# Dividing a seven-tap convolution between four engines in another way, in a fused convolution and gated-FFN kernel

**Chip, cores, metric.** One core of one Trainium2 chip. The metric is device time in microseconds (us) of one execution, first to last instruction of the core plus 1.7 to 1.9 us that the profile's span doesn't hold (785.21 us against a span of 783.3 in the kernel before). All runs quoted are fast (granted TensorE clock 0.98 or more, no outlier).

## The reference

```python
# x: (8, 4096, 192), weight: (8, 7), w_gate and w_val: (192, 1536), w_out: (1536, 192); all float32
w   = softmax(weight, axis=-1)                       # 8 heads x 7 taps
xc  = causal_conv_along_seq(x, w)                    # per head (24 channels), 6 zeros ahead of each batch row
xc  = xc.reshape(32768, 192)
g   = xc @ w_gate
out = (g * sigmoid(g) * (xc @ w_val)) @ w_out        # float32, (32768, 192)
```

## The kernel before

The 32768 tokens are 64 blocks of 512, four blocks to a unit, so 16 units (0 to 15). A block is 12 steps, j = 0 to 11; a step makes one gate and one val tile of 128x512 on TensorE, a SiLU of gate on ScalarE, h = SiLU x val on VectorE. At j = 1, 4, 7 and 10 TensorE also runs a phase of the down projection, which eats the h tiles of earlier steps.

The convolution of a unit is done ahead of its use, in one of two ways. Some units are convolved on TensorE, as matmuls with a banded matrix. The units in `POOLED` are convolved "channel-major": their input is cast to fp16 in DRAM (`xs`), loaded transposed (`x<-xs`, channels on partitions), and the seven taps become per-partition multiplies and adds, shared by VectorE, ScalarE and GpSimd. Each such unit has six jobs: four "block" jobs for channels 0 to 127 and two "pair" jobs for channels 128 to 191 of two blocks. Four placing copies for each block then put the result where TensorE reads it (`pxc`).

```python
POOLED = (3, 4, 5, 7, 8, 9, 11, 12, 13, 15)
...
    def turn_x(u, i, at):                       # a transposing load, on SyncE's queue
        rows = xs[u][TB * i : TB * i + TB + XP]
        ...
        t = cpool.tile([P, TB + XP], fp16, tag=tag, name=tag, bufs=6)     # rings of six: x0 and x64
        seq(nc.sync.dma_start_transpose(out=t, in_=rows[:, at : at + P]))
...
    SHARES = (                                  # taps on VectorE, ScalarE, GpSimd; jobs alternate
        ((0, 1), (2, 3, 4), (5, 6)),
        ((0, 1, 2), (3, 4), (5, 6)),
    )
...
            for k in pool_taps:                 # GpSimd: a multiply and an add for each of its taps
                part = cpool.tile([P, TB], fp32, tag="piece", name="piece", bufs=2)
                seq(nc.gpsimd.tensor_tensor(part, shifted(k),
                        job["tap"][:, k : k + 1].to_broadcast([P, TB]), op=ALU.mult))
                add(part, k)
...
    def place(u, i):                            # four copies on SyncE's queue
        t0, t1, t2 = xc[b]
        y = y2[u, i % 2][Q * (i // 2) : Q * (i // 2) + Q, :]
        for dst, src in (
            (t1[0:Q, 0:TB], t0[Q:P, 0:TB]), (t1[Q:P, 0:TB], y),
            (t2[0:Q, 0:TB], y), (t2[Q:P, 0:TB], t0[0:Q, 0:TB]),
        ):
            seq(nc.sync.dma_start(out=dst, in_=src))
...
    def pooled_work(n, room):                   # room: j in (1, 7, 10) and no TensorE convolution in this step
        if room:
            if on_dve: on_dve.pop(0)()          # one VectorE tap and one ScalarE tap of the oldest jobs
            if on_act: on_act.pop(0)()
        while placing: ...                      # place(u, i) once its jobs are 12 steps old
...
        silu[n] = seq(nc.scalar.activation(sg, g, AF.Silu)).ins           # in each step
        hj = hpool.tile([P, TB], fp16, tag="h", name="h", bufs=15)
        seq(nc.vector.tensor_tensor(hj, sg, v, op=ALU.mult))
...
            seq(nc.scalar.copy(o_sb[:, 0:2, :], acc[b][0]))               # at j = 4, then the store on SyncE
            seq(nc.vector.tensor_copy(o_sb[:, 2:4, :], acc[b][1]))
```

## Time and profile before

| | before |
|---|---|
| median (range) of the four runs beside the changed kernel | 787.86 us (784.68 to 788.2) |
| span of the profiled run, clock | 783.3 us, 1.00 |
| TensorE work of a block when nothing waits | 11.73 us |
| lost beyond that: blocks 0 to 5 / blocks 6 to 62 | 10.5 / 8.0 us |

The two last rows come from the start of the first gate matmul of each block. "Lost" is the distance between two such starts minus 11.73 us. The prediction shows the page's busy row, chain and main groups. Two more groups of that page matter for the move of the copies (columns: line, engine, operation, tiles, shapes, count | busy us, mean ns | idle before):

```profile
L778 DVE TENSOR_TENSOR h<-sig,val 128x512 f16<-128x512 f16 x768 | 498.7, 683 | 67.5 <-PE val L767 49.1
...
L852 DVE COPY o_sb<-acc 128x384 f32<-128x384 f32 x63 | 34.5, 548 | 0.0
L851 ACT COPY o_sb<-acc 128x384 f32<-128x384 f32 x63 | 30.2, 479 | 0.2
```

VectorE has h in every step, all its taps and one of two output copies, and is idle 67.5 us in 783 before h. TensorE's waits for other engines, the largest first (us in total, times, longest), are all short:

```profile
PE cv L462 <- DMA x<-x: 1.3, 1, 1.3
...
PE acc L793 <- DVE h L778: 0.7, 1, 0.7
```

### The profile page before, as it was taken

Reading aid. Unit: us, or ns where it says so; the run is one execution under the profiler, and the core shown is the slowest. Engines: PE = TensorE matmul, PEld = TensorE weight load, DVE = VectorE, ACT = ScalarE, POOL = GpSimd, SP = SyncE. Lnnn points to the kernel's source line nnn. Section 1 sums busy time; section 2 is a strip of 40 time slices with the busy share of each in tenths; the row PEclk is TensorE's granted clock in tenths of the full one; section 3 lists DMA queues with packets and bytes.
Section 4 is the critical chain, followed back from the end, with each engine's and each line's share of the span. In section 5 each row is a group of like instructions: output and inputs, shape, how many; then the busy total and the mean of one; then the engine's idle time right before and its main releaser. Section 6 shows DMA issues by size and latency. Waiting matters only on the chain.

```text
span 783.3 us, 28008 instructions
## 1 busy us (share of the span) xinstructions
PE 773.8 (99%) x11371; PEld 583.4 (74%) x11371; DVE 705.2 (90%) x1042; ACT 596.4 (76%) x1022; POOL 539.1 (69%) x459
## 2 busy tenths in 40 slices
PE   8999999999999999999999999999999999999998
PEld 5676667987888768888888866676787886666665
DVE  7676999999999989999999999999999988997775
ACT  6665877877877878778778778778787777786664
POOL 8200488988998769879899858788889965783000
PEclk9999999999999999999999999999999999999999
DMA  9996676652185465454156548555224753521211
GB/s 139 157 183 133 139 137 103 137 118 77 52 153 111 102 153 95 103 131 111 36 100 137 102 108 156 107 124 104 73 64 77 168 123 94 108 65 36 69 56 42
DMA packets 159803, 83.91 MB, mean 107 GB/s; under 512 B 102513, under 2 KB 159097, under 8 KB 159097
## 3 DMA queue, kind: packets, MB, share of 16 engines
q1 hardware_dynamic: 139144, 65.57, 36.5%
q0 software_dynamic: 20528, 16.55, 15.2%
q8 instruction: 89, 1.46, 0.8%
q14 instruction: 42, 0.34, 0.1%
HBM read 33.09 MB, written 38.60 MB: 92 GB/s over the span
## 4 chain that ended last, share of the span: by engine, by line
PE 93%; SPq 3%; DMA 2%; DVE 1%; issue 1%; POOL 1%; ACT 0%; DVEq 0%; POOLq 0%
PE gate L767 35%; PE acc L793 31%; PE val L767 26%; SPq L498 1%; SPq L520 1%; DMA x<-x 1%; DMA w<-in_moe_w_val_dram 1%; DVE h L778 1%; PE cv L462 1%; SPq L598 1%; POOL w L168 0%; PE acc L814 0%; POOL xe L98 0%; PE cv L373 0%; PE turn L431 0%
## 5 line engine op out<-in xcount | busy, mean ns | idle before, releaser
L776 ACT ACTIVATE sig<-gate 128x512 f16<-128x512 f32 x768 | 458.5, 597 | 168.0 <-PE val L767 76.7
L778 DVE TENSOR_TENSOR h<-sig,val 128x512 f16<-128x512 f16 x768 | 498.7, 683 | 67.5 <-PE val L767 49.1
L767 PEld LDWEIGHTS <-w 64*128 64x128 f16 x4608 | 317.4, 110 | 145.2 <-issue 3.1
L767 PE MATMUL gate<-pxc,w 64*128 64x512 f16 x1440 | 338.5, 376 | 0.0
L767 PE MATMUL val<-pxc,w 64*128 64x512 f16 x1440 | 337.0, 376 | 0.4
L793 PE MATMUL acc<-wo,h 64*128 64x192 f16 x6096 | 318.3, 243 | 0.7 <-DVE h L778 0.7
L793 PEld LDWEIGHTS <-h 64*128 64x128 f16 x6096 | 287.0, 94 | 39.5 <-issue 2.2
L634 POOL TENSOR_TENSOR total<-total,part 128x512 f32<-128x512 f32 x150 | 198.4, 1323 | 106.6 <-DVE total L668 69.8
L767 PE MATMUL gate<-xc,w 64*128 64x512 f16 x864 | 203.8, 376 | 0.5 <-ACT tap_c L567 0.5
L767 PE MATMUL val<-xc,w 64*128 64x512 f16 x864 | 203.5, 376 | 0.7 <-DMA w<-in_moe_w_val_dram 0.3
L649 POOL TENSOR_TENSOR piece<-x,tap_c 128x512 f32<-128x512 f16 x120 | 143.6, 1197 | 0.0
L681 ACT ACTIVATE part<-x,tap_c 128x512 f32<-128x512 f16 x150 | 107.1, 714 | 0.0
L668 DVE SCALAR_TENSOR_TENSOR total<-x,tap_c,total 128x512 f32<-128x512 f16 x90 | 93.5, 1038 | 0.0
L634 POOL TENSOR_TENSOR total<-total,piece 128x512 f32<-128x512 f32 x60 | 80.4, 1340 | 4.7
L668 DVE SCALAR_TENSOR_TENSOR total<-x,tap_c,fill 128x512 f32<-128x512 f16 x60 | 80.1, 1334 | 0.0
L634 POOL TENSOR_TENSOR pxc<-total,piece 128x512 f16<-128x512 f32 x40 | 54.3, 1358 | 3.1
L490 POOL COPY tm<-tm 128x1280 f16<-128x1280 f16 x5 | 6.2, 1250 | 41.4 <-DVE tm L479 41.4
L852 DVE COPY o_sb<-acc 128x384 f32<-128x384 f32 x63 | 34.5, 548 | 0.0
L851 ACT COPY o_sb<-acc 128x384 f32<-128x384 f32 x63 | 30.2, 479 | 0.2
L634 POOL TENSOR_TENSOR y<-total,piece 128x512 f16<-128x512 f32 x20 | 27.4, 1372 | 1.6
L98 POOL DMA_DIRECT2D x<-in_x_dram x16 | 12.6, 808 | 12.4 <-ACT sig L776 12.4
L479 ACT CAST tm<-cv 128x480 f16<-128x480 f32 x20 | 10.2, 562 | 8.9 <-PE cv L462 8.9
(68 smaller groups left out, 89.7 us busy)
## 6 DMA issues: line engine op xcount, KB each, us to landing
out_dram<-o_sb SPq DMA_DIRECT2D x63, 384.0 KB
xs<-in_x_dram POOLq DMA_DIRECT2D x7, 774.0 KB, 7.2
pxc<-pxc SPq DMA_DIRECT2D x80, 64.0 KB
pxc<-y SPq DMA_DIRECT2D x80, 64.0 KB
scr<-tm SPq DMA_DIRECT2D x35, 130.0 KB
x<-in_x_dram POOLq DMA_DIRECT2D x8, 480.0 KB, 9.3
x<-x SPq DMA_DIRECT2D x8, 480.0 KB
xs<-in_x_dram POOLq DMA_DIRECT2D x3, 768.0 KB, 7.8
```

The costliest lines, as they stand in the source:

```text
L98: nc.gpsimd.dma_start(out=t[p0 + i0 : p0 + i1, w0 - at : w1 - at, :], in_=bass.AP(tensor=x_flat.tensor, offset=(t0 + size * w0 - pad + i0) ...
L479: eng(tm[u][:, NG * r : NG * r + NG, 2 * grp * hp : 2 * grp * hp + 2 * grp].rearrange("p g (t e) -> p g t e", t=2), banks[r][:, 0 : 2 * w] ...
L634: nc.gpsimd.tensor_tensor(job["dst"] if k == K - 1 else total, total, part, op=ALU.add)
L649: nc.gpsimd.tensor_tensor(part, shifted(k), job["tap"][:, k : k + 1].to_broadcast([P, TB]), op=ALU.mult,)
L668: nc.vector.scalar_tensor_tensor(total, x_k, job["tap"][:, k : k + 1], other, op0=ALU.mult, op1=ALU.add,)
L681: nc.scalar.activation(part, shifted(k), AF.Copy, scale=job["tap"][:, k : k + 1])
L767: nc.tensor.matmul(o, w16[m][p0 : p0 + Q, k, e::E], xc[b][k][p0 : p0 + Q, 0:TB], start=(k == 0), stop=(k == SL - 1),)
L776: silu[n] = seq(nc.scalar.activation(sg, g, AF.Silu)).ins
L778: seq(nc.vector.tensor_tensor(hj, sg, v, op=ALU.mult))
L793: nc.tensor.matmul(acc[b][bank][:, s, :], hj[p0 : p0 + Q, ts(2 * bank + s, P)], wo16[p0 : p0 + Q, j, :], start=(not second and j == 0 and ...
L851: seq(nc.scalar.copy(o_sb[:, 0:2, :], acc[b][0]))
L852: seq(nc.vector.tensor_copy(o_sb[:, 2:4, :], acc[b][1]))
```

## The change

Its intent is to take load off VectorE, give GpSimd a cheaper multiply and a steadier pace, and convert one more unit. The taps of a job are dealt anew: ScalarE makes the first sum (tap 0) and one part, VectorE adds two taps, GpSimd multiplies and adds three. VectorE's taps may now stand at j = 4 as well. Both output copies go to ScalarE. Units 2, 6, 10 and 14 come in and 5, 9 and 13 go out, with hand-set times for units 2 and 3.

```diff
-    POOLED = (3, 4, 5, 7, 8, 9, 11, 12, 13, 15)
+    POOLED = (2, 3, 4, 6, 7, 8, 10, 11, 12, 14, 15)
...
+    FIRST, ON_DVE, ON_ACT, ON_POOL = 0, (1, 2), (3,), (4, 5, 6)
...
-            for k in pool_taps:
+            for k in ON_POOL:
                 part = cpool.tile([P, TB], fp32, tag="piece", name="piece", bufs=2)
                 seq(
-                    nc.gpsimd.tensor_tensor(
-                        part,
-                        shifted(k),
-                        job["tap"][:, k : k + 1].to_broadcast([P, TB]),
-                        op=ALU.mult,
+                    nc.gpsimd.tensor_scalar(
+                        part, shifted(k), scalar1=job["tap"][:, k : k + 1],
+                        scalar2=1.0, op0=ALU.mult, op1=ALU.mult,
                     )
                 )
                 add(part, k)
...
+            if k == FIRST:                      # ScalarE opens the job: total = tap_0 * x
...
+                part = job["total"] = cpool.tile(
+                    [P, TB], fp32, tag="total", name="total", bufs=5
+                )
+                dve_steps.extend((index, lambda k=k: dve_step(k)) for k in ON_DVE)
...
+        cast, jobs = {2: (19, 44), 3: (40, 60)}.get(v, (s0 - 118, s0 - 95))
+        turns = (
+            (0, 0), (0, Q), (2, Q), None, (1, 0), (1, Q), (3, Q), None, (2, 0), (3, 0)
+        )
+        lead = {2: (33, 1), 3: (49, 1)}.get(v, (cast + 7, 2))
...
+            if ready is not None and (
+                j in (4, 10) or (j in (1, 7) and ready < ahead)
+            ):
+                dve_steps.pop(0)[1]()
+            if j in (1, 7, 10) and act_steps and (ready is None or ahead < ready + 3):
+                act_steps.pop(0)[1]()
...
-            if n < max(max(finished[job] for job in need) + 12, ustep * u + NCH * i - 16):
+            if n < max(done + 14, ustep * u + NCH * i - 16):
...
-            seq(nc.vector.tensor_copy(o_sb[:, 2:4, :], acc[b][1]))
+            seq(nc.scalar.copy(o_sb[:, 2:4, :], acc[b][1]))
```

Also cut: the channel taps' two copies out of PSUM become one.

More of the change, by code (lines that the diff above doesn't have):

```diff
@@ L556, in make_channel_taps @@
     def make_channel_taps():
-        for name in pick:
-            bank = ppool.tile([P, TB], fp32, tag="gate", name="ctap")
+        bank = ppool.tile([P, TB], fp32, tag="gate", name="ctap")
+        for m, name in enumerate(pick):
             for a in range(2):
@@ L561, in make_channel_taps @@
                     nc.tensor.matmul(
-                        bank[:, 0:K], pick[name], split[:, a, 0:K, 0],
-                        start=(a == 0), stop=(a == 1),
-                    )
-                )
-            taps[name] = small(f"tap_{name}", [P, K])
-            seq(nc.scalar.copy(taps[name], bank[:, 0:K]))
+                        bank[:, m * K : m * K + K], pick[name], split[:, a, 0:K, 0],
+                        start=(m == 0 and a == 0), stop=(a == 1),
+                        skip_group_check=True,
+                    )
+                )
+        both_taps = small("both_taps", [P, 2 * K])
+        seq(nc.scalar.copy(both_taps, bank[:, 0 : 2 * K]))
+        for m, name in enumerate(pick):
+            taps[name] = both_taps[:, m * K : m * K + K]
     def cast_x(u):
@@ L602, in join_x, with conv_job @@
         seq(nc.sync.dma_start(out=x12[u, i + 2][0:Q], in_=x12[u, i][Q:P]))
-    SHARES = (
-        ((0, 1), (2, 3, 4), (5, 6)),
-        ((0, 1, 2), (3, 4), (5, 6)),
-    )
-    on_dve = []
-    on_act = []
-    finished = {}
-    started = []
-    def conv_job(n_job, u, what, i):
-        dve_taps, act_taps, pool_taps = SHARES[n_job % len(SHARES)]
-        job = {"dve": len(dve_taps), "act": len(act_taps), "parts": []}
-        at = XP - pad
-        def open_job():
-            if what == "pair":
-                y2[u, i] = cpool.tile([P, TB], fp16, tag="y2", name="y2", bufs=4)
-                job.update(dst=y2[u, i], src=x12[u, i + 2], tap=taps["c2"])
-            else:
-                t = cpool.tile([P, XW], fp16, tag="pxc0", name="pxc0", bufs=8)
-                xc[UB * u + i] = [t]
-                job.update(dst=t[:, 0:TB], src=x01[u, i], tap=taps["c01"])
-            job["total"] = cpool.tile([P, TB], fp32, tag="total", name="total", bufs=4)
+    FIRST, ON_DVE, ON_ACT, ON_POOL = 0, (1, 2), (3,), (4, 5, 6)
+    act_steps = []
+    dve_steps = []
+    finished = {}
+    n_jobs = [0]
+    step_now = [0]
+    def conv_job(u, what, i):
+        index = n_jobs[0]
+        n_jobs[0] += 1
+        job = {"dve": len(ON_DVE), "act": len(ON_ACT), "parts": []}
+        at = XP - pad
         def shifted(k):
@@ L656, in proceed @@
                 add(part, k)
-            finished[u, what, i] = True
+            finished[u, what, i] = step_now[0]
         def dve_step(k):
-            if "total" not in job:
-                open_job()
-            total, x_k, other = job["total"], shifted(k), job["total"]
-            if k == 0:
-                total = total.rearrange("p (s e) -> p s e", s=SUBS)
-                x_k = x_k.rearrange("p (s e) -> p s e", s=SUBS)
-                other = fill.unsqueeze(1).to_broadcast([P, SUBS, P])
             seq(
                 nc.vector.scalar_tensor_tensor(
-                    total, x_k, job["tap"][:, k : k + 1], other,
+                    job["total"], shifted(k), job["tap"][:, k : k + 1], job["total"],
                     op0=ALU.mult, op1=ALU.add,
@@ L676, in act_step @@
         def act_step(k):
-            if "total" not in job:
-                open_job()
-            part = cpool.tile([P, TB], fp32, tag="part", name="part", bufs=6)
+            if k == FIRST:
+                if what == "pair":
+                    y2[u, i] = cpool.tile([P, TB], fp16, tag="y2", name="y2", bufs=4)
+                    job.update(dst=y2[u, i], src=x12[u, i + 2], tap=taps["c2"])
+                else:
+                    t = cpool.tile([P, XW], fp16, tag="pxc0", name="pxc0", bufs=8)
+                    xc[UB * u + i] = [t]
+                    job.update(dst=t[:, 0:TB], src=x01[u, i], tap=taps["c01"])
+                part = job["total"] = cpool.tile(
+                    [P, TB], fp32, tag="total", name="total", bufs=5
+                )
+                dve_steps.extend((index, lambda k=k: dve_step(k)) for k in ON_DVE)
+            else:
+                part = cpool.tile([P, TB], fp32, tag="part", name="part", bufs=6)
+                job["parts"].append((part, k))
             seq(
@@ L684, in act_step @@
             )
-            job["act"] -= 1
-            job["parts"].append((part, k))
-            proceed()
-        on_dve.extend(lambda k=k: dve_step(k) for k in dve_taps)
-        on_act.extend(lambda k=k: act_step(k) for k in act_taps)
+            if k != FIRST:
+                job["act"] -= 1
+                proceed()
+        act_steps.extend((index, lambda k=k: act_step(k)) for k in (FIRST, *ON_ACT))
     def place(u, i):
@@ L711 @@
     plan = {}
-    jobs_made = []
     placing = []
     def queue_jobs(u):
-        for what, i in (
+        for job in (
             ("block", 0), ("pair", 0), ("block", 1), ("pair", 1),
@@ L719, in queue_jobs @@
         ):
-            conv_job(len(jobs_made), u, what, i)
-            jobs_made.append((u, what, i))
+            conv_job(u, *job)
         placing.extend((u, i) for i in range(UB))
@@ L725, in planned, with pooled_work @@
         s0 = ustep * v
-        plan.setdefault(s0 - 118, []).append(lambda: cast_x(v))
-        for off, i, at in (
-            (-111, 0, 0), (-110, 0, Q), (-109, 2, Q), (-103, 1, 0),
-            (-102, 1, Q), (-101, 3, Q), (-94, 2, 0), (-85, 3, 0),
-        ):
-            plan.setdefault(s0 + off, []).append(lambda i=i, at=at: turn_x(v, i, at))
-        for off, i in ((-106, 0), (-98, 1)):
-            plan.setdefault(s0 + off, []).append(lambda i=i: join_x(v, i))
-        plan.setdefault(s0 - (86 if v == POOLED[0] else 95), []).append(lambda: queue_jobs(v))
-    def pooled_work(n, room):
-        if room:
-            if on_dve:
-                on_dve.pop(0)()
-            if on_act:
-                on_act.pop(0)()
+        cast, jobs = {2: (19, 44), 3: (40, 60)}.get(v, (s0 - 118, s0 - 95))
[3 more added lines that the diff above has]
+        lead = {2: (33, 1), 3: (49, 1)}.get(v, (cast + 7, 2))
+        plan.setdefault(cast, []).append(lambda: cast_x(v))
+        for m, turn in enumerate(turns):
+            if turn:
+                todo = lambda turn=turn: turn_x(v, *turn)
+            else:
+                todo = lambda i=m // 4: join_x(v, i)
+            plan.setdefault(lead[0] + lead[1] * m, []).append(todo)
+        plan.setdefault(jobs, []).append(lambda: queue_jobs(v))
+    def pooled_work(n, j, busy):
+        step_now[0] = n
+        if not busy:
+            ready = dve_steps[0][0] if dve_steps else None
+            ahead = act_steps[0][0] if act_steps else n_jobs[0]
+            if ready is not None and (
[4 more added lines that the diff above has]
+                act_steps.pop(0)[1]()
         while placing:
@@ L744, in pooled_work @@
             need = (u, "block", i), (u, "pair", i % 2)
-            for job in need:
-                if finished.get(job) is True:
-                    finished[job] = n
             if not all(job in finished for job in need):
                 break
-            if n < max(max(finished[job] for job in need) + 12, ustep * u + NCH * i - 16):
+            done = max(finished[job] for job in need)
+            if n < max(done + 14, ustep * u + NCH * i - 16):
                 break
@@ L924 @@
             job()
-        pooled_work(n, j in (1, 7, 10) and not work)
+        pooled_work(n, j, work is not None)
         if u + 1 < NU and not pooled(u + 1):
```

## The prediction

Its sum stands, 793.4 us of span, and its terms can be followed but for the last: the + 2, the clock after the long wait, as no trace had shown it. Without that term the sum is 791.4. The 0.7 us for the new multiply is the author's estimate from the GpSimd copy of 128x1280 (1.25 us).

> **What bounds the kernel now.** I read the page first (busy shares, chain of waits), then the groups, the waits with the DMA queue's own, then single stretches of the timeline. The page gives the bound at once:
>
> ```profile
> PE 773.8 (99%) x11371; PEld 583.4 (74%) x11371; DVE 705.2 (90%) x1042; ACT 596.4 (76%) x1022; POOL 539.1 (69%) x459
> ...
> PE 93%; SPq 3%; DMA 2%; DVE 1%; issue 1%; POOL 1%; ACT 0%; DVEq 0%; POOLq 0%
> ```
>
> TensorE is busy for 99% of the 783.3 us and is 93% of the chain. A block is 12 steps; a step is one gate/val pair and its share of the down projection. In the chain in order of time one phase of the block (36 down matmuls) returns at a fixed pitch:
>
> ```profile
> 99.13 1.48 PE acc L793 x36
> 110.86 1.48 PE acc L793 x36
> 122.59 1.49 PE acc L793 x36
> ```
>
> 110.86 - 99.13 = 11.73 us for a block, 0.978 us for a step. No change here touches this work, so 11.73 is the floor. From the first gate matmuls of all 64 blocks in the trace: the first is at 8.46, the last at 766.00, and 63 x 11.73 = 739.0 of the 757.5 between. So only 18.5 us of PE loss exist between the first block and the last (whose 17.35 us hold the tail). They lie so: 7.6 in blocks 0 to 2 (start-up, two matmul convolutions for unit 1, channel taps); 2.9 in blocks 4 and 5 (convolution of unit 2); 1.5, 1.8 and 1.7 for units 6, 10, 14; 1.0 in block 42; some 2 in four clusters of about 0.5, where DVE was full. Faster by 2% would need 15.8 us of these 18.5.
>
> The convolution of unit 2, in TensorE's timeline, with its wait for the row copy:
>
> ```profile
> 73.70 0.27 PE L462 MATMUL cv<-x,band 64*32 64x240 f16 x1
> 75.31 0.60 PE L462 MATMUL cv<-x,band 64*32 64x240 f16 x31 [1.34 <-DMA x<-x]
> ```
>
> The channel-major work costs (groups; last column is idle time before):
>
> ```profile
> L634 POOL TENSOR_TENSOR total<-total,part 128x512 f32<-128x512 f32 x150 | 198.4, 1323 | 106.6 <-DVE total L668 69.8
> L649 POOL TENSOR_TENSOR piece<-x,tap_c 128x512 f32<-128x512 f16 x120 | 143.6, 1197 | 0.0
> L681 ACT ACTIVATE part<-x,tap_c 128x512 f32<-128x512 f16 x150 | 107.1, 714 | 0.0
> L668 DVE SCALAR_TENSOR_TENSOR total<-x,tap_c,total 128x512 f32<-128x512 f16 x90 | 93.5, 1038 | 0.0
> ```
>
> The queue that carries all SyncE transfers is in order. In two waits it already stands behind GpSimd, harmlessly; and its rows show what one set of four placing copies costs:
>
> ```profile
> SPq L855 <- DVE o_sb L852: 270.5, 36, 28.3
> ...
> SPq L598 <- POOL piece L649: 7.0, 6, 2.6
> ```
> ```profile
> 190.78 0.46 SPq L706 DMA_DIRECT2D pxc<-pxc  x1
> 191.30 1.26 SPq L706 DMA_DIRECT2D pxc<-y  x2
> 192.61 0.59 SPq L706 DMA_DIRECT2D pxc<-pxc  x1
> ```
>
> Their last packet ends at 194.3, so 1.7 us from issue to data. A transposing load takes 1.26 us of the queue (median of 80).
>
> [...] the copy of 128x1280 took 1.25 us, so I estimate 0.6 to 0.8 us for the new multiply, 0.7 in the sums. [...] the same DVE add takes from 0.736 to 1.854 us. [...]
>
> **The change, part by part.**
>
> *Eleven channel-major units instead of ten; 2 in, and 6, 10, 14 in for 5, 9, 13.* Five matmul convolutions become four. Removed: unit 2's, 2.9 us with its wait. The other three move, at about 1.6 each.
>
> *Channel taps*: two banks and two copies become one; the 0.75 us of step 33 shrinks. -0.3.
>
> *A job.* Before, on average 2.5 DVE steps (2.9 us with the dearer first one), 2.5 ACT (1.8), on GpSimd 4.5 adds x 1.335 + 2 multiplies x 1.197 = 8.4 us. After: 2 DVE (2.1), 2 ACT (1.4), GpSimd 4 x 1.335 + 3 x 0.7 = 7.4 us. The code emits a job every 6 or 9 steps, 8 on average = 7.8 us, instead of 10. GpSimd holds that pace as long as the multiply is under 0.83.
>
> *Output copies.* DVE loses 63 x 0.55 = 34.5 us, ACT gains 63 x 0.48 = 30. By block in full stretches: DVE 12 x 0.65 + 3 x 1.04 = 10.9 of 11.73 (before, full); ACT 12 x 0.597 + 3 x 0.714 + 2 x 0.48 = 10.3. Neither binds on average, and the four clusters should go: -1.5. But at j = 4 ACT now has two copies before the next SiLU and DVE a tap; the down phase at j = 7 wants h of j = 5 about 1.8 us after. I see about no margin left when the DVE add is contended: +1 in all.
>
> *What I hold for decisive: buffers of the early units.* Unit 2's jobs are emitted from step 46, unit 3's from 94 and unit 4's from 142 (in steady state units are two ahead, here one). But unit 4's loads keep the general timing, steps 81 to 99, with six x0 buffers in a ring and four a unit. Counting the ring: unit 4's blocks 0 to 3 take over unit 2's blocks 2, 3 and unit 3's 0, 1. In the built program the load of unit 4's block 3 (step 99) does wait for DVE's tap at step 118 and for the third GpSimd multiply of that job (unit 3, block 1). Behind it in the same queue stand an output store and the four placing copies of unit 2's block 2, which step 120 reads.
>
> From the start of step 118: 0.65 until its val is complete, 0.1, h 0.65, add 1.0: DVE's second tap is done at 2.4. GpSimd: 3 adds x 1.335 + 3 multiplies x 0.7 = 6.1, so 8.5. Load 1.26, store 0.5, four copies at about 0.6: last issued at 12.2, landed at 13.9. Step 120 starts 2.78 after 118 (step 118 has the 1.485 us down phase) and needs the last copies 0.43 later, at 3.2. PE waits 10.7 us, once. Hardly anything in it can shrink by more than 1 or 2 us.
>
> The same, weaker, at step 108: load of unit 4's block 1 waits for the job of step 94 (8.5), three loads (3.9), copies, landed at 16.0 after step 94; the need is at 14.9: +1.1. [...] Later units have their loads at least 9 steps behind the freeing jobs.
>
> Sum: 783.3 - 2.9 - 0.3 - 1.5 + 1.0 + 1.1 + 10.7 + 2 = 793.4 us of span. The profiled run's time was 1.9 above its span: 795.
>
> **The rivals.** (1) *The queue does not hold PE*: then 783.3 - 2.9 - 0.3 - 1.5 (+1) = 778.6 to 779.6, time about 781. For it: before, such waits sum to 7.0 us and cost nothing; someone who set units 2 and 3 by hand may have looked at unit 4. Against it: the order in the queue and the two semaphores are in the program, and the early units have no lead. (2) *GpSimd becomes the bound*: with a multiply of 1.2 us a job is 8.9 us against 7.8, over 18 jobs 20 us behind; the five sums and six parts then run out and ScalarE stops in front of a SiLU; step 120's wait grows by 9 to about 20 us: 805 to 812. For it: the old multiply took 1.2. [...] (3) *ScalarE and DVE bursts*: 0.3 us lost in each of some 47 loaded blocks, 14 us, on top. Against it: before, DVE was full in these blocks and PE lost 2 us in all[...].
>
> **Range and chances.** Predicted 795 us. The low end 780 is rival 1; the high end 806 has half of rival 2 or 3 on top. Faster by 2% (under 772.4) needs almost all losses gone: 0.02. Slower by 2% (over 804) needs a second mechanism: 0.10. Within: 0.88.
>
> **What would show it.** Right: one TensorE gap of 9 to 12 us at about 134 us before a gate matmul of step 120, ended by a pxc copy; SyncE's wait for piece or total much above 7.0 us, with a transposing load just before the copies; lower PEclk in that slice; blocks of 11.73 elsewhere; no cv wait for a row copy; GpSimd's multiply 0.6 to 0.8; DVE busy near 640. Wrong: no gap there (rival 1); new GpSimd multiplies over 1 us and ScalarE waiting for GpSimd (rival 2); many gaps of 0.2 to 0.7 us at j = 7 before acc, for DVE's h (rival 3).

## The result, and the profile after

| | before | after |
|---|---|---|
| median of four runs (range) | 787.86 us (784.68 to 788.2) | 808.68 us (807.77 to 809.68) |
| ratio of the fast runs | 1 | 1.0274, 95% interval 1.0244 to 1.0303 |
| span of the profiled run | 783.3 us | 807.9 us |

The change makes the kernel 2.7% slower. A ratio here is the mean time of one kernel's fast runs over that of the other's of the same rounds, so not quite the ratio of the medians. The output is correct.

Busy work of the page after, and the chain:

```profile
PE 781.0 (97%) x11307; PEld 546.9 (68%) x11307; DVE 644.9 (80%) x957; ACT 594.9 (74%) x1062; POOL 545.3 (67%) x521
...
PEclk9999998799999999999999999999999999999999
...
PE 90%; POOL 3%; DVE 2%; SPq 1%; issue 1%; DMA 1%; ACT 0%; DVEq 0%; POOLq 0%; ACTq 0%
```

VectorE has become freer by 60 us (705.2 to 644.9) and it did not help. TensorE's busy share falls from 99% to 97%, and it is busy for 7 us longer with fewer matmuls: some of them ran at half clock (0.50 in the clock record). The clock row, in 40 slices of 20.2 us, dips in slices 7 and 8 only (121 to 162 us). TensorE's waits:

```profile
PE gate L766 <- DMA pxc<-pxc: 13.1, 2, 10.1
PE acc L792 <- DVE h L777: 6.2, 18, 0.5
```

So two long waits for placing copies, and eighteen short ones for h in the down phase. Both are new. Time lost beyond 11.73 us a block, from the first gate matmuls (us):

| | first gate matmul at | blocks 0 to 3 | 4, 5 | 6 to 8 | 9 | 10 | 11 to 62 | last, with tail |
|---|---|---|---|---|---|---|---|---|
| before | 8.46 | 7.61 | 2.92 | 0.00 | 0.00 | 0.00 | 8.01 | 5.62 |
| after | 9.62 | 6.67 | 1.72 | 0.41 | 6.70 | 12.69 | 13.68 | 5.70 |
| difference | +1.16 | -0.94 | -1.20 | +0.41 | +6.70 | +12.69 | +5.67 | +0.08 |

The differences add up to the 24.6 us of the spans. Nearly four fifths (19.4 us) lie in blocks 9 and 10.

**Blocks 9 and 10.** SyncE's queue around them (start, us, engine line operation, tiles, how many; several of one kind in a row are one line):

```profile
113.22 3.76 SPq L601 DMA_TRANSPOSE x<-xs  x3
120.30 0.48 SPq L605 DMA_DIRECT2D x<-x  x1
...
121.59 3.81 SPq L601 DMA_TRANSPOSE x<-xs  x3
125.45 0.59 SPq L700 DMA_DIRECT2D pxc<-pxc  x1
...
128.99 20.74 SPq L601 DMA_TRANSPOSE x<-xs  x2
149.78 0.58 SPq L854 DMA_DIRECT2D out_dram<-o_sb  x1
150.42 0.50 SPq L700 DMA_DIRECT2D pxc<-pxc  x1
150.96 1.34 SPq L700 DMA_DIRECT2D pxc<-y  x2
152.34 0.59 SPq L700 DMA_DIRECT2D pxc<-pxc  x1
```

Of the two top lines, L605 is the join copy of a unit's rows between two `x` tiles; it stood from 117.04 to 120.27 us for an earlier load to land. The line at 128.99 is two transposing loads with a wait of nearly 20 us between them: the second needs a buffer that a late job still reads. The output store and the four copies behind it were free to go, but the queue is in order: they went out from 149.78 us on, right behind the second load. What the loads in the queue waited for, from the queue's own list of waits over the whole run (times and longest after the sum):

```profile
SPq L601 <- POOL piece L641: 18.8, 12, 6.1
SPq L601 <- DVE total L651: 12.4, 1, 12.4
```

and TensorE at the end of the two waits (the bracket is its idle time and what ended it):

```profile
127.49 0.58 PE L766 MATMUL gate<-pxc,w 64*128 64x512 f16 x1 [2.93 <-DMA pxc<-pxc]
...
153.10 0.58 PE L766 MATMUL gate<-pxc,w 64*128 64x512 f16 x1 [10.13 <-DMA pxc<-pxc]
```

The wait before step 120 closes almost to a ring: the load waits for a VectorE tap and a GpSimd multiply, these are only reached when TensorE has got into step 118, the copies wait behind the load, and TensorE needs the copies for step 120, two steps on. The matmuls take 0.58 us there, where 0.38 is usual: after each wait TensorE runs at half clock (0.50 in the clock record, from 126.49 to 133.32 us and from 146.97 to 157.21). Of block 10's 12.69 us 10.13 are the wait and 2.56 the cold clock and what else the restart costs.

**The short waits.** One of the eighteen ends at 199.40 us. The timeline of the kernel after, all engines in order of start:

```profile
196.62 0.48 ACT L851 COPY o_sb<-acc 128x384 f32<-128x384 f32 x1
...
196.92 1.27 POOL L626 TENSOR_TENSOR pxc<-total,piece 128x512 f16<-128x512 f32 x1
196.99 1.75 DVE L651 SCALAR_TENSOR_TENSOR total<-x,both_taps,total 128x512 f32<-128x512 f16 x1
196.99 1.79 ACT L775 ACTIVATE sig<-gate 128x512 f16<-128x512 f32 x3
...
198.66 1.27 DVE L777 TENSOR_TENSOR h<-sig,val 128x512 f16<-128x512 f16 x2
...
199.40 0.34 PE L792 MATMUL acc<-wo,h 64*128 64x192 f16 x4 [0.41 <-DVE h L777]
```

ScalarE finishes its second copy at 197.1 and its next three SiLU take 1.79 us together, so the first is done at about 197.6, and with it the input of h. But VectorE took the tap of j = 4 first, and that tap lasted 1.75 us instead of its shortest, 0.74, because GpSimd's add had begun 0.07 us earlier. (In this trace 70 taps begin inside a GpSimd add with 0.1 us or more of it left, and all end 0.55 to 0.64 us after it; the 20 taps beside no GpSimd instruction take 0.74 to 0.75. All 132 take from 0.74 to 2.41, 0.94 in the median.) h starts at 198.66, and the down phase at j = 7 waits 0.41 us for it.

**GpSimd.** The groups of its new multiply and of VectorE's taps after:

```profile
L641 POOL TENSOR_SCALAR piece<-x,both_taps 128x512 f32<-128x512 f16 x198 | 164.1, 829 | 0.0
...
L651 DVE SCALAR_TENSOR_TENSOR total<-x,both_taps,total 128x512 f32<-128x512 f16 x132 | 140.4, 1064 | 0.0
```

The multiply costs 829 ns on average instead of 1197. Its median is 692; beside a VectorE tap it takes some 1.13 us. A job lasts 7.3 to 8.9 us on GpSimd, 8.1 in the median.

### The profile page after: what moved, and what is told of

It reads as the page before. It is cut to its first block, busy times and chain, and to the rows that moved or that the text cites. A ratio compares the mean times of both kernels' runs of the same rounds, so it can differ in the third digit from the quotient of the medians.

```text
span 807.9 us, 27770 instructions
## 1 busy us (share of the span) xinstructions
PE 781.0 (97%) x11307; PEld 546.9 (68%) x11307; DVE 644.9 (80%) x957; ACT 594.9 (74%) x1062; POOL 545.3 (67%) x521
## 4 chain that ended last, share of the span: by engine, by line
PE 90%; POOL 3%; DVE 2%; SPq 1%; issue 1%; DMA 1%; ACT 0%; DVEq 0%; POOLq 0%; ACTq 0%
PE gate L766 45%; PE acc L792 28%; PE val L766 14%; DVE h L777 2%; POOL total L626 2%; POOL piece L641 1%; DMA x<-xs 1%; PE warm L867 1%; PE cv L462 1%; SPq L601 0%; SPq L520 0%; PE turn L431 0%; POOL pxc L626 0%; DMA pxc<-pxc 0%; PE cv L373 0%
## 5 line engine op out<-in xcount | busy, mean ns | idle before, releaser
L766 PEld LDWEIGHTS <-w 64*128 64x128 f16 x4608 | 281.7, 110 | 186.0 <-issue 20.0
L766 PE MATMUL gate<-pxc,w 64*128 64x512 f16 x1584 | 374.6, 378 | 13.2 <-DMA pxc<-pxc 13.1
L766 PE MATMUL val<-pxc,w 64*128 64x512 f16 x1584 | 373.8, 378 | 0.2
L626 POOL TENSOR_TENSOR total<-total,piece 128x512 f32<-128x512 f32 x132 | 175.9, 1333 | 11.0
L766 PE MATMUL gate<-xc,w 64*128 64x512 f16 x720 | 169.8, 376 | 0.0
L641 POOL TENSOR_SCALAR piece<-x,both_taps 128x512 f32<-128x512 f16 x198 | 164.1, 829 | 0.0
L626 POOL TENSOR_TENSOR total<-total,part 128x512 f32<-128x512 f32 x66 | 87.7, 1328 | 79.4 <-DVE total L651 49.3
L651 DVE SCALAR_TENSOR_TENSOR total<-x,both_taps,total 128x512 f32<-128x512 f16 x132 | 140.4, 1064 | 0.0
L676 ACT ACTIVATE total<-x,both_taps 128x512 f32<-128x512 f16 x66 | 47.1, 714 | 2.6 <-DMA x<-xs 2.6
L676 ACT ACTIVATE part<-x,both_taps 128x512 f32<-128x512 f16 x66 | 47.1, 713 | 0.0
```

The source lines that it names most:

```text
L626: nc.gpsimd.tensor_tensor(job["dst"] if k == K - 1 else total, total, part, op=ALU.add)
L641: nc.gpsimd.tensor_scalar(part, shifted(k), scalar1=job["tap"][:, k : k + 1], scalar2=1.0, op0=ALU.mult, op1=ALU.mult,)
L651: nc.vector.scalar_tensor_tensor(job["total"], shifted(k), job["tap"][:, k : k + 1], job["total"], op0=ALU.mult, op1=ALU.add,)
L676: nc.scalar.activation(part, shifted(k), AF.Copy, scale=job["tap"][:, k : k + 1])
L766: nc.tensor.matmul(o, w16[m][p0 : p0 + Q, k, e::E], xc[b][k][p0 : p0 + Q, 0:TB], start=(k == 0), stop=(k == SL - 1),)
```

## The experiments

The theories. A: what is lost in blocks 9 and 10 is SyncE's queue, where unit 4's loads, waiting for buffers, stand ahead of placing copies. D: the eighteen waits at j = 7 come from VectorE's tap at j = 4. Their rivals (any other letter in an expectation is one of these): GpSimd is too slow for its jobs, so that the copies are late whatever the queue does; and ScalarE's two copies at j = 4 hold up the SiLU. Each kernel was correct. The kernel before had medians of 786.15, 786.62 and 786.51 us in the three sittings (e1 to e4, e5 to e8, e9 and e10), each on another chip; so runs of different sittings are compared by their ratios. Spans and lost time are those of one profiled execution for each kernel.

| run | median us | ratio to before, 95% interval | span | lost in 0 to 3 / 4, 5 / 6 to 8 / 9 / 10 / 11 to 62 |
|---|---|---|---|---|
| e1_x0_ten | 793.93 | 1.0089 (1.0067 to 1.0112) | 789.4 | 6.84 / 1.49 / 0.85 / 2.45 / 0.04 / 12.47 |
| e2_unit4_late | 791.16 | 1.0065 (1.0040 to 1.0089) | 789.8 | 8.49 / 1.94 / 0.73 / 0.36 / 0.00 / 13.42 |
| e3_tap_off_j4 | 800.29 | 1.0187 (1.0156 to 1.0218) | 798.8 | 6.66 / 2.39 / 4.80 / 0.90 / 13.61 / 4.43 |
| e4_copy_dve | 821.0 | 1.0441 (1.0426 to 1.0457) | 819.1 | 7.01 / 2.37 / 1.56 / 3.44 / 14.03 / 25.77 |
| e5_all | 786.84 | 1.0000 (0.9969 to 1.0030) | 786.3 | 7.38 / 0.00 / 5.11 / 0.00 / 0.00 / 8.06 |
| e6_unit2_mm | 788.39 | 1.0029 (1.0004 to 1.0053) | 787.0 | 6.73 / 5.75 / 0.00 / 1.83 / 0.00 / 7.77 |
| e7_old_multiply | 814.21 | 1.0356 (1.0332 to 1.0380) | 813.5 | 6.73 / 0.92 / 4.78 / 0.00 / 0.00 / 35.39 |
| e8_all_copy_dve | 787.16 | 0.9999 (0.9964 to 1.0034) | 786.2 | 7.88 / 1.53 / 6.03 / 0.00 / 0.00 / 5.66 |
| e9_unit3_late | 782.9 | 0.9961 (0.9943 to 0.9979) | 781.1 | 7.20 / 0.00 / 1.15 / 0.00 / 0.00 / 7.37 |
| e10_plain_start | 785.48 | 0.9989 (0.9969 to 1.0009) | 784.0 | 6.74 / 6.13 / 0.00 / 0.00 / 0.00 / 6.01 |

### e1: ten buffers for the block loads

```diff
-        t = cpool.tile([P, TB + XP], fp16, tag=tag, name=tag, bufs=6)
+        t = cpool.tile([P, TB + XP], fp16, tag=tag, name=tag, bufs=(10, 6)[at // Q])
```

> Edit: ten x0 buffers instead of six, nothing else. Theory A (unit 4's early loads wait for a buffer and hold the placing copies behind them in the in-order queue): both gaps, before step 108 and step 120, vanish, with the half clock after them; those two blocks cost 6.7 + 12.7 = 19.4 us over 11.73 each, so 808.7 - 19.4 = 789 us (787 to 792). Rival B (GpSimd is the bound and the queue only reports it): with jobs that come late anyway, at most 3 us are won, 805 or more, and the gap before step 120 stays.

The order in the queue is as before the edit, but the loads have no buffer to wait for. The wait of 10 us is gone and block 10 loses 0.04 us. The span falls by 18.5 us to 789.4, with no other engine made faster. This profiled execution was the fastest of the four; the median, 793.93, lies above the 787 to 792 expected. So GpSimd's pace did not make the copies of block 10 late: the load ahead of them did. Block 9 still loses 2.45 us: the loads wait for no buffer now, but three of them, and a join copy that waits 1.45 us for a load to land, still stand ahead of its copies.

### e2: unit 4's loads later, in the same six buffers

```diff
-        lead = {2: (33, 1), 3: (49, 1)}.get(v, (cast + 7, 2))
+        lead = {2: (33, 1), 3: (49, 1), 4: (112, 2)}.get(v, (cast + 7, 2))
```

> Edit: six buffers kept, unit 4's loads moved from steps 81-99 to steps 112-130. Theory A: the copies no longer stand behind a load that waits, so as with ten buffers 789 us (787 to 793), with no gap before steps 108 and 120. Rival C (more buffers helped for another reason, not by the order in the queue): still over 800.

Same gain as e1 from the other side: the loads still need their buffers, but are issued when these are free. Blocks 9 and 10 lose 0.36 us together, against 19.39 after the change. Theory A holds, with the time that the loads take in the queue as a part of it. Both runs keep 12 to 13 us of loss in blocks 11 to 62, so the waits at j = 7 are another matter.

### e3: no VectorE tap at j = 4

```diff
-                j in (4, 10) or (j in (1, 7) and ready < ahead)
+                j in (1, 7, 10)
```

> Edit: VectorE's taps at phases 1, 7, 10 of a block instead of 4, 10 and at times 1, 7; every job's second tap stays at its step. Theory D (the tap at phase 4, when it is held up by a GpSimd add, makes h of phase 5 late for the down phase at 7): the 18 waits of PE for h, 6.2 us, vanish: 802 to 804 us, the gaps at 108 and 120 as before. Rival E (ScalarE's two output copies make the SiLU of phase 5 late): the waits stay, 807 to 809.

TensorE's waits for h in the down phase, 18 before this edit, are gone. The list now begins with:

```profile
PE gate L766 <- DMA pxc<-pxc: 13.5, 2, 11.3
```

Blocks 11 to 62 lose 4.43 us instead of 13.68, so the taps at j = 4 had cost 9.25 us in these traces. (The median, 800.29, is below the 802 to 804 expected.) ScalarE still has its two copies at j = 4, so these were not the cause. Theory D holds. The long wait of block 10 stays; that of block 9 goes (0.90), but 4.80 us appear in blocks 6 to 8, a first sign of what e5 ran into.

### e4: the second output copy back on VectorE, taps still at j = 4

```diff
-            seq(nc.scalar.copy(o_sb[:, 2:4, :], acc[b][1]))
+            seq(nc.vector.tensor_copy(o_sb[:, 2:4, :], acc[b][1]))
```

> Edit: the second output copy back on VectorE, taps as in the change. Theory D: VectorE has 0.55 us more at phase 4, so PE's waits for h at phase 7 grow in number and length, 809 to 818 us. Rival E: with one copy less ahead of the SiLU the waits vanish, 802 to 804.

The waits for h more than double, in number and in time:

```profile
PE acc L792 <- DVE h L777: 17.5, 39, 0.8
```

The span rises by 11.2 us, and the median of 821.0 is above the 809 to 818 expected. If ScalarE's two copies had been the trouble, this would have been faster. A copy (0.55 us) put in front of h on VectorE is one more delay of the same kind as the tap.

### e5: the three mends together

```diff
        (the edits of e1, e2 and e3)
```

> Edit: ten x0 buffers, unit 4's loads at steps 112-130, taps at phases 1, 7, 10, together. If the waits behind unit 4's loads (19.4 us) and behind the tap of phase 4 (6 to 9 us) are all that the change loses, the span is 807.9 - 19.4 - 8 = 780.5, time 780 to 783, faster than before (784.7 to 788) by 0.5 to 1%. If they hide something else (GpSimd behind by then, the queue of the first units) 786 or more.

The time is 786.84 us, the same as before the change, not the 780 to 783 expected: a miss, though with a wide spread (782.02 to 789.86, so the fastest of six runs was as expected). Blocks 9 and 10 are clean, and nothing is lost in blocks 4 and 5 in this execution. But 5.11 us are lost in block 8: TensorE waits 2.44 us for a copy at step 96, then runs at half clock from 115.44 to 118.85. The queue ahead of that step in e5:

```profile
100.31 8.35 SPq L601 DMA_TRANSPOSE x<-xs  x2
108.76 0.53 SPq L854 DMA_DIRECT2D out_dram<-o_sb  x1
...
110.64 0.56 SPq L700 DMA_DIRECT2D pxc<-pxc  x1
```

Two of unit 3's loads occupy 8.35 us (5.72 and 2.58), where a load usually takes 1.26 (median of 88), and unit 2's first placing copies stand behind them. The four runs with e3's edit and unit 3's loads in their old place (e3, e5, e7, e8) all lose 4.8 to 6.0 us in blocks 6 to 8, the four others of this set of units 0.4 to 1.6; how the taps' place leads to it is not shown. Some of the gain is also missing in blocks 11 to 62, which lose 8.06 us against 4.43 in e3; three waits for h at j = 5, 1.9 us together, are part of it.

### e6: e5 with the old set of channel-major units

```diff
-    POOLED = (2, 3, 4, 6, 7, 8, 10, 11, 12, 14, 15)
+    POOLED = (3, 4, 5, 7, 8, 9, 11, 12, 13, 15)
```

> Edit: as the one with all three mends, but with the units of before (unit 2, 6, 10 and 14 on TensorE, 5, 9 and 13 channel-major). My term for unit 2, 2.9 us, says 2 to 3 us slower than with all mends. If the early channel-major unit costs as much by its own waits (its first load is late at step 49, 1 to 2.4 us) as its matmuls did, the two are equal within 1 us.

Inconclusive. The hand-set times for units 3 and 4 belong to the new set. With the old one ScalarE waits 3.4 us for a load at step 64 and 2.7 at step 118, and TensorE behind it 2.4 and 1.5 us for a SiLU; a stretch of half clock follows the first (mean granted clock of the run 0.997). Blocks 4 and 5 lose 5.75 us together and block 9 1.83. The worth of unit 2 cannot be read from this run; e10 repeats it with fitting times.

### e7: e5 with the old multiply on GpSimd

```diff
-                    nc.gpsimd.tensor_scalar(
-                        part, shifted(k), scalar1=job["tap"][:, k : k + 1],
-                        scalar2=1.0, op0=ALU.mult, op1=ALU.mult,
+                    nc.gpsimd.tensor_tensor(
+                        part, shifted(k),
+                        job["tap"][:, k : k + 1].to_broadcast([P, TB]),
+                        op=ALU.mult,
```

> Edit: as the one with all three mends, but GpSimd multiplies by tensor_tensor with a broadcast tap, as before. At 4 x 1.33 + 3 x 1.2 = 8.9 us a job against a pace of 7.8, GpSimd falls 1.1 us a job behind: if buffers then stop ScalarE, 5 to 25 us slower than with all mends, with ScalarE's sums or parts waiting for GpSimd; if the slack of 5 sums and 14 steps is enough, within 2 us of it.

27 us slower than e5, just above the 5 to 25 expected. GpSimd falls behind, and ScalarE stands still in front of a SiLU. ScalarE's wait for a load, and the largest wait of TensorE:

```profile
ACT total L677 <- DMA x<-xs: 13.0, 2, 10.7
...
PE acc L793 <- ACT sig L776: 10.2, 2, 9.5
```

It was expected that sums or parts would run out, and they did not; no wait of ScalarE for GpSimd is in the list. GpSimd also issues the casts of `x` to DRAM. Here it came to the one for a later unit only at 211.95 us (199.91 in e5); SyncE's load of that unit waited for it from 204.69 to 218.61, ScalarE's first tap waited 10.68 us for the load, and TensorE 9.47 us for the SiLU behind that tap. Placing copies that stood behind loads in SyncE's queue cost TensorE another 5.41 and 2.69 us (waits from 330.09 and 528.82).

The multiply takes 1154 ns here against 849 in e9. So the new multiply is needed for three GpSimd taps a job, and the prediction's rival 2 was a real danger that the change avoids, though on another path than the one it named.

### e8: e5 with the second output copy on VectorE

```diff
        (the edit of e4, on top of e5)
```

> Edit: as the one with all three mends, but the second output copy on VectorE. VectorE then has 12 x 0.65 + 3 x 1.06 + 0.55 = 11.5 us a block of 11.73: if only the tap at phase 4 was the harm, within 1.5 us of all mends; if VectorE has no room left, 3 to 10 us slower, with PE's waits for h at phases 5 and 7.

786.2 us of span, 0.9999 by ratio: no difference from e5 that these runs can show. Where no tap stands at j = 4, it doesn't matter which engine copies. In e4 the same edit cost 11 us.

### e9: e5 with unit 3's last two loads behind the copies

```diff
+            late = 27 + 2 * (m - 8) if v == 3 and m > 7 else 0
-            plan.setdefault(lead[0] + lead[1] * m, []).append(todo)
+            plan.setdefault(lead[0] + lead[1] * m + late, []).append(todo)
```

> The combined kernel with unit 3's last two transposing loads moved from steps 57 and 58 to steps 84 and 86, behind the placing copies of unit 2's block 0; the jobs that read them come only at steps 127 and 133. Theory (what kept the combined kernel from its gain is the full queue before step 96): TensorE's 2.44 us wait for pxc at 113.4 us and the half clock after it, together the 5.1 us lost in block 8, go; nothing else moves; span 786.3 - 5.1 = 781.2, time 780 to 783, ratio to the kernel before 0.992 to 0.995. Rival (those two loads only happened to be in the queue; the copies are late because GpSimd's job is): block 8 still loses 4 to 5 us, time 786 to 788, ratio 1.000.

The span is 781.1 against 781.2 expected; the ratio, 0.9961, is a little above the 0.992 to 0.995 expected. The queue of e9 at the same place:

```profile
107.84 0.50 SPq L700 DMA_DIRECT2D pxc<-pxc  x1
...
110.35 2.57 SPq L601 DMA_TRANSPOSE x<-xs  x2
```

The copies are issued 2.8 us earlier, and the two loads now take 2.57 us together. Blocks 6 to 8 lose 1.15 instead of 5.11. This is the fastest kernel, 0.39% below before (interval 0.21 to 0.57%); the interval just overlaps that of e5, so the gain over e5 rests on the traces as much as on the times.

What made those loads slow is not gone, only out of the way. In e9 the queue stands still just ahead of these lines too, from 97.06 to 105.38 us, with a join copy that waits for a load to land. In both runs GpSimd's cast of another unit is then on its way to DRAM (issued at 97.1 in e5 and 96.6 in e9, landed at 105.6 and 105.5). This is a pattern of all twelve traces: each of the 32 loads that hold the queue for more than 4.4 us begins while such a cast is under way and ends between 2.0 us before and 0.6 us after its landing; with none under way no load takes more than 3.9 us. No run moved a cast, so why loads and casts meet like this stays open.

### e10: e5 with the old set of units and plain times

```diff
-    POOLED = (2, 3, 4, 6, 7, 8, 10, 11, 12, 14, 15)
+    POOLED = (3, 4, 5, 7, 8, 9, 11, 12, 13, 15)
-        cast, jobs = {2: (19, 44), 3: (40, 60)}.get(v, (s0 - 118, s0 - 95))
+        cast, jobs = {3: (26, 58)}.get(v, (s0 - 118, s0 - 95))
-        lead = {2: (33, 1), 3: (49, 1), 4: (112, 2)}.get(v, (cast + 7, 2))
+        lead = (cast + 7, 2)
```

> The combined kernel with the old set of channel-major units (3 to 5, 7 to 9, 11 to 13, 15), the old start of unit 3's jobs at step 58 and the general timing of all loads: the new division of the work without unit 2's conversion, and so without its early crush on the queue. Theory: no wait for pxc at all; the matmul convolution of unit 2 costs its 2.9 us again (wait of 1.3 for the row copy in it) and nothing else differs: span near 781.2 + 2.9 = 784, time 784 to 786, ratio 0.997 to 1.000, that is 0.3 to 0.5% above the run with unit 3's loads late. Rival (converting unit 2 gains nothing even when the queue is in order, as its work on ScalarE and the queue costs as much): time 780 to 783, same as the other run or below.

The span is the 784.0 expected, but partly by chance. Unit 2's matmul convolution loses 6.13 us here in blocks 4 and 5, not 2.92, partly as its rows come later:

```profile
74.68 0.26 PE L462 MATMUL cv<-x,band 64*32 64x240 f16 x1 [0.95 <-DMA x<-x]
76.65 1.00 PE L462 MATMUL cv<-x,band 64*32 64x240 f16 x31 [1.71 <-DMA x<-x]
```

These two waits are also followed by half clock, from 76.08 to 79.50 us, some 1.7 us lost; the kernel before, with one wait of 1.34 us, kept its full clock there. Against that, e9 loses 1.15 us in blocks 6 to 8 and 1.36 more in blocks 11 to 62. Net, e9 is 2.9 us shorter by span and 0.28% by ratio, and the two intervals just overlap. Converting unit 2 is worth some 2 to 3 us once the queue is in order; these runs do not fix it closer.

## Why the prediction was wrong

It said 795 us (780 to 806); the median is 808.68. The mechanism of its largest loss was right, and it named that loss to within a few hundredths, so closely only by luck: the wait was 10.13 us and not 10.7, the rest 2.56 and not 2. Two other terms of its sum were mis-sized, and two small ones. It gave a time above 804 us a chance of 0.10, as that needed a second mechanism; these two terms together went past it.

| term | predicted | measured (from the table of lost time) |
|---|---|---|
| wait before step 120, with cold clock | 10.7 + 2 | 12.69 |
| wait before step 108 | 1.1 | 6.70, and 0.41 in blocks 6 to 8 |
| relief of VectorE, and bursts at j = 4 and 7 | -1.5 + 1.0 | +5.67 |
| unit 2's convolution | -2.9 | -1.20 |
| start, channel taps, blocks 0 to 3, tail | -0.3 | +0.30 |
| sum | 10.1 | 24.6 |

**The wait before step 120 was right.** The order of the queue, the load in it that waits for VectorE's tap of step 118, the store and copies behind it: the trace has each of them. Counted from the start of step 118 at 139.66 us, VectorE's tap is done at 2.8 (predicted 2.4), GpSimd's third multiply at 8.9 (8.5) and the last copy is issued at 13.3 (12.2). e1 and e2 remove the loss by removing the load's wait.

**"Load of unit 4's block 1 waits for the job of step 94 (8.5)" failed.** The order in the queue was right and the times were not. It let GpSimd begin that job when VectorE's taps were done. VectorE was done at 112.6 us in the trace; GpSimd was still in the job before and began at 114.5, 1.9 us late. Jobs come in bursts, pairs 6 steps (5.9 us) apart, and each lasts about 8.1 us; the prediction used the mean spacing of 8 steps (7.8 us), by which GpSimd keeps up. It does so on average but not inside a burst. VectorE's tap was itself 0.8 us later than the 2.4 after step 94's start (109.45) that the prediction assumed. So the job's third multiply ended 11.4 us after that start and not 8.5.

The sum also left out two waits ahead in the queue: unit 4's first load stood for a buffer until 113.19 us, and the join copy then 3.23 us for a load to land. The queue came to the load of block 1 only at 121.47, 0.66 us after its buffer was free, so GpSimd's late job was not the only hold. (In e1, with no buffer to wait for, this load goes out 9.9 us after step 94's start, here 12.1.) The last copies were issued by 127.95, and TensorE went on with all it needed at 128.8, where the prediction's 16.0 us after step 94 come to 125.5.

The prediction also gave this wait, 1.1 us in its sum, no cold clock. Its own trace had one wait of 1.34 us at full clock and none longer, so what a longer one does was not shown. A recorded idle time of 2.93 us was enough (columns: us, then busy time and instructions of PE, PEld, DVE, ACT, POOL, then granted clock, DMA share, GB/s):

```profile
129.40:131.40 2.00, 2.00 (x15) 1.23 (x16) 0.69 (x1) 1.10 (x3) 0.92 (x1) 0.50 0.45 96
...
133.40:135.00 1.60, 1.60 (x19) 0.96 (x17) 0.58 (x1) 1.16 (x2) 1.56 (x2) 1.00 0.00 0
```

The trace's clock record has half clock from 126.49 to 133.32 us, so it begins 1.93 us into that idle time; TensorE was at work for nearly 6 us of that stretch, so some 2.9 us were lost. In the wait of 10.13 us half clock begins at 146.97, 4.00 us into the idle time, and lasts to 157.21, with TensorE at work for the last 4.1 us. These changes of the clock lie 6.83, 13.65 and 10.24 us apart, which is 2, 4 and 3 times 3.41; the stretches of half clock in e5 and e10 last 3.41 and 3.42. In e5 the clock dropped 2.05 us after the end of an idle time of 2.44, in e10 inside one of 1.71 that followed one of 0.95. What sets the moment of a drop is not shown.

**"+1 in all" for the bursts failed.** The place was right (j = 4 and j = 7, h of j = 5), but the sum gave it +1 us over all 47 loaded blocks. Eighteen waits of up to 0.5 us appear, 6.2 us in all, and e3 shows that the taps at j = 4 cost 9.25 us of span with all that follows. The argument against rival 3, that VectorE had been full before and PE lost only 2 us, weighed the total load and not the place: before, no tap stood at j = 4. The load fell, but a tap moved into the one slot with a deadline about 1.8 us off. The trace before already had such an add of VectorE last from 0.736 to 1.854 us. In the trace after, the tap begun 0.07 us after the start of a 1.27 us add ended 0.55 us after the add, in the range of those 70 taps (0.55 to 0.64). By these figures a tap at j = 4 is to be counted at up to some 1.8 us (1.27 + 0.55), and not at its mean of 1.04.

**Unit 2's term (-2.9) came only in part.** e5 and e9 have 0.00 in blocks 4 and 5. In the changed kernel these blocks still lose 1.72 us, and 0.92 to 2.39 in the six other runs with these units (e7 and e8 load them as e5 does, so no mend explains the 0.00). ScalarE waits there 2.6 us for unit 2's first load, and TensorE 1.1 us for a SiLU behind it.

**Rivals.** Rival 1 (the queue does not hold PE, 781) was wrong for this kernel. e9, with the queue in order and no tap at j = 4, has a span of 781.1, close to that rival's 779.6. Rival 2 did not happen because the multiply took 0.83 us on average, just at the limit that the prediction named; e7 shows what a slower one would have cost. Rival 3 happened in part, and its sign, short waits at j = 7 for h, was the one seen.

## What to carry to other kernels

In an in-order queue, look at each transfer that may wait for a buffer and ask what stands behind it that could have gone: two load times or four more buffers were worth some 15 to 18 us here, where the whole change, once mended (e9), gains about 3. Count an engine's work by its deadline and not by its average: a tap in the slot before a needed result cost 9 us on an engine that had just been given 60 us of rest. And when work is moved early to the start of a program, its loads, its copies and the steady state's loads meet in the same queue, so check the first units one by one. Nor is an engine's pace all that it gives: in e7 the late GpSimd cost most by a cast that it issued late.
